# Layout changes of attention scores and probabilities: from VectorE block transposes to DMA transposes on SyncE's queue

## The chip, the cores and the metric

The kernel runs on one core of a Trainium2 chip. The metric is the device time of one execution in microseconds (us), by the slowest core, which here is the only one. An execution over 1.5% above the fastest of the same kernel counts as disturbed; undisturbed runs are compared throughout.

## The reference

The inputs are 2048 positions of 1024 features in bf16. Three things are computed from the same x and mixed by a gate of one value per position:

```python
def reference(A_x, A_wqkv, A_wo, B_x, B_w_gate, B_w_up, B_w_down, gate_w):
    # attention: 32 heads of 32, window of 8 positions, 2 apart (0, 2, .. 14 back)
    qkv = ...(x @ wqkv)                                  # 1024 -> 3 x 1024
    logits = einsum("bhsd,bhswd->bhsw", q, kg) * scale   # 8 logits per position and head
    attn = softmax(where(mask, logits, -1e9))
    a = einsum("bhsw,bhswd->bhsd", attn, vg) @ wo
    # feed-forward, 1024 -> 3584 -> 1024
    b = (gelu(x @ w_gate) * (x @ w_up)) @ w_down
    g = sigmoid((x * gate_w).sum(-1, keepdims=True))
    return g * a + (1 - g) * b
```

All weight products are large matrix products for TensorE. The window attention has only 8 logits per position and head, so it is done by VectorE, element by element.

## The kernel before

The positions come in four chunks of 512 (chunks 0 and 1 make the first half of the run, 2 and 3 the second), and the attention of each chunk in two halves of 256 (h = 0 to 7). Queries, keys and values lie as 128 partitions (32 heads times 4) by positions. VectorE multiplies and adds them to the partial scores of a half, 128 x 2048 values in bf16. The softmax wants positions on the partitions, so the scores are transposed, and the probabilities are transposed back before they multiply the values:

```python
# att_half: one half of a chunk
o = dve(2.24, taking("z", lambda: nc.vector.transpose(out=flat("z"), in_=xbuf[:, accs[h], :])), [("qk", h)],
        pre=xb_pre(), key=("acct", h))                       # scores: one "whole" transpose
# ... fold: adds the 4 partial sums of a head (VectorE), mask, maximum, subtraction
def exps():                                                  # ScalarE
    if a == 0:
        nc.scalar.activation(out=gates[c][0][:], in_=gates[c][2][:], func=ACT.Exp)
    nc.scalar.activation(out=lsb(), in_=lsb(), func=ACT.Exp, scale=scale)
# ... sums, reciprocal, gate (VectorE); spread: each probability copied 4 times (ScalarE)
for i in range(2):
    def back(i=i):                                           # probabilities: a pair of half-size transposes
        nc.vector.transpose(out=flat("ab")[:, i * n // 2:(i + 1) * n // 2],
                            in_=flat("e")[:, i * n // 2:(i + 1) * n // 2])
# ... products with V and their sums (VectorE), which write the attention output
```

All of this is woven into the matrix work of TensorE by a small scheduler that runs while the kernel is built. It gives every operation of each engine its place in a fixed order, from costs that it assumes. For transfers it assumes a common pipe and 2.2 us on top:

```python
LAT = 0.1
RATE = 340e3
...
if op.eng in ("SP", "POOL"):              # SyncE's and GpSimd's transfers
    nbytes, issue = op.cost
    self.clk[op.eng] = t + issue
    self.pipe = max(self.pipe, t) + nbytes / self.RATE
    op.end = self.pipe + 2.2
```

An engine that waits for one operation holds up all that stands behind it in its order; the lines below show it (ScalarE stands 8.04 us for one operation of VectorE's, with a copy behind it that TensorE needs). ScalarE's order holds the attention's exponentials and spreads as well as copies out of TensorE's result banks ("evacuations"); VectorE's order too. SyncE issues nearly all loads, in order: weights into a ring of 20 slots, and x by transposing loads. GpSimd issues the stores of computed weight combinations, 28 of "dforms", 8 of "oforms" and 56 of "fforms", nearly all in the first 230 us, and most outputs.

The loads of x for chunk 3 go into the buffer of chunk 0's values, so they wait for chunk 0's attention, and they stand in SyncE's order among the weights:

```python
xs = [... for z in lend[0:4]]             # x of chunk 3 lies in lend[3]
vT = [lend[3], lend[5], lend[1], lend[5]] # V of chunk 0 lies in lend[3]
def load_x(c, deps):
    deps = deps + ([[("acct", 1)], [("att", 0)]][c - 2] if c > 1 else [])
...
for b in range(2, NBLK):
    yield from load_block(0, b)
    if b >= XB:
        for c, k0 in ((2, 0), (2, 4), (3, 0), (3, 4))[b - XB:b - XB + 1]:
            yield from list(load_x(c, []))[k0:k0 + 4]
```

## Time and profile before

| | before |
|---|---|
| time, median of 3 (lowest to highest) | 732.13 us (731.79 to 732.85) |
| profiled span | 729.7 us |
| TensorE busy | 721.8 us, 99% |
| VectorE busy | 631.6 us, 87% |
| ScalarE, GpSimd busy | 314.9 us, 72.0 us |
| TensorE's clock granted | 1.00 |

The page of a profile has the busy time of each engine, then a row per engine of 40 slices of the span (here 18.2 us each) whose digits are busy tenths. "Busy" includes a matmul that runs slowly (for the same 3397 matmuls TensorE is busy 721.8 us before and 726.8 us after), so busy has to be compared with the matmuls' distance in time, as the prediction does. The lines themselves are shown in the prediction.

### The profile page before, as it was taken

Reading aid. Unit: us, or ns where it says so; the run is one execution under the profiler, and the core shown is the slowest. Engines: PE = TensorE matmul, PEld = TensorE weight load, DVE = VectorE, ACT = ScalarE, POOL = GpSimd, SP = SyncE. Lnnn points to the kernel's source line nnn. Section 1 sums busy time; section 2 is a strip of 40 time slices with the busy share of each in tenths; the row PEclk is TensorE's granted clock in tenths of the full one; section 3 lists DMA queues with packets and bytes.
Section 4 is the critical chain, followed back from the end, with each engine's and each line's share of the span. In section 5 each row is a group of like instructions: output and inputs, shape, how many; then the busy total and the mean of one; then the engine's idle time right before and its main releaser. Section 6 shows DMA issues by size and latency. Waiting matters only on the chain.

```text
span 729.7 us, 9971 instructions
## 1 busy us (share of the span) xinstructions
PE 721.8 (99%) x3397; PEld 356.0 (49%) x3397; DVE 631.6 (87%) x935; ACT 314.9 (43%) x532; POOL 72.0 (10%) x128
## 2 busy tenths in 40 slices
PE   8999999999999999999999998999999999999998
PEld 5666644444444444456665444444444444444443
DVE  2689999999999989999899999999999999969300
ACT  2333455558555561035652113576557654220110
POOL 2234422121210100000000001000000000001000
PEclk9999999999999999999999999999999999999999
DMA  9999965648892869943029999555455544899992
GB/s 302 333 325 363 380 200 170 187 139 212 213 227 74 280 194 326 314 162 116 29 89 300 358 302 333 165 150 155 147 159 147 156 151 145 303 304 336 323 303 104
DMA packets 151507, 163.73 MB, mean 224 GB/s; under 512 B 22944, under 2 KB 112032, under 8 KB 151456
## 3 DMA queue, kind: packets, MB, share of 16 engines
q1 hardware_dynamic: 142624, 135.30, 60.1%
q0 software_dynamic: 8544, 27.27, 10.1%
q8 instruction: 26, 0.43, 0.2%
q10 hardware_dynamic: 288, 0.52, 0.2%
q14 instruction: 25, 0.20, 0.1%
HBM read 129.50 MB, written 28.31 MB: 216 GB/s over the span
## 4 chain that ended last, share of the span: by engine, by line
PE 73%; issue 21%; DVE 2%; ACT 1%; DMA 1%; POOL 1%; POOLq 0%; ACTq 0%
PE ps L970 44%; PE ps L1117 17%; PE ps L473 11%; DVE xbuf L922 1%; POOL out_dram L1144 1%; DMA hT<-in_A_x_dram 0%; DVE xbuf L930 0%; PE ps L1212 0%; DMA out_dram<-ost 0%; DVE xbuf L935 0%; DVE ost L1191 0%; ACT ost L1152 0%; ACT L1058 0%; DVE xbuf L787 0%; PE ps L717 0%
## 5 line engine op out<-in xcount | busy, mean ns | idle before, releaser
L970 PEld LDWEIGHTS <-ring 128*128 128x128 bf16 x1568 | 153.2, 98 | 187.7 <-issue 3.5
L970 PE MATMUL ps<-lend,ring 128*128 128x512 bf16 x896 | 212.3, 379 | 2.2 <-ACT m L1024 2.1
L970 PE MATMUL ps<-tf,ring 128*128 128x512 bf16 x672 | 164.0, 379 | 0.0
L1117 PE MATMUL ps<-ring,hT 128*128 128x512 bf16 x708 | 160.7, 379 | 0.0
L1117 PEld LDWEIGHTS <-hT 128*128 128x128 bf16 x708 | 69.2, 98 | 83.3
L781 DVE TENSOR_TENSOR xbuf<-qo,lend 128x2048 bf16<-128x2048 bf16 x64 | 77.4, 1218 | 2.1 <-ACT lend L495 2.1
L922 DVE TENSOR_TENSOR xbuf<-xbuf,lend 128x2048 bf16<-128x2048 bf16 x64 | 77.4, 1218 | 0.1
L787 DVE TENSOR_TENSOR xbuf<-xbuf 128x2048 bf16<-128x2048 bf16 x56 | 68.2, 1218 | 0.2
L609 PEld LDWEIGHTS <-ring 128*128 128x128 bf16 x336 | 44.0, 131 | 28.7 <-DMA ring<-in_A_wqkv_dram 0.4
L473 PE MATMUL ps<-lend,ring 128*128 128x512 bf16 x256 | 56.3, 381 | 0.1
L1042 ACT ACTIVATE gl<-ps 128x512 bf16<-128x512 f32 x56 | 33.5, 598 | 51.5 <-PE ps L970 51.4
L999 ACT COPY ps<-ps 128x512 f32<-128x512 f32 x56 | 32.0, 571 | 54.9 <-PE ps L970 54.8
L1152 ACT ACTIVATE ost<-ps,omg 128x512 bf16<-128x512 f32 x16 | 11.0, 688 | 102.5 <-PE ps L1117 99.3
L1144 POOL DMA_DIRECT2D out_dram<-ost x24 | 13.0, 540 | 413.4 <-ACT ost L1152 319.4
L1117 PE MATMUL ps<-ring,qo 128*128 128x512 bf16 x192 | 49.3, 379 | 0.0
L473 PEld LDWEIGHTS <-ring 128*128 128x128 bf16 x256 | 36.8, 145 | 19.0 <-issue 0.7
L443 POOL DMA_DIRECT2D fforms<-ring x56 | 30.4, 544 | 132.4 <-DVE ring L435 120.6
L609 PE MATMUL ps<-lend,ring 128*128 128x512 bf16 x192 | 43.5, 379 | 0.0
L1014 DVE TENSOR_TENSOR hT<-hT,gl 128x1024 bf16<-128x1024 bf16 x56 | 38.4, 686 | 5.8 <-ACT hT L1011 4.5
L930 DVE TENSOR_TENSOR xbuf<-xbuf 128x1024 bf16<-128x1024 bf16 x64 | 41.9, 686 | 0.7
L1054 DVE TENSOR_TENSOR u<-ps,u 128x512 f32<-128x512 f32 x56 | 38.4, 686 | 4.6 <-PE ps L970 3.4
L1033 DVE TENSOR_TENSOR hT<-ps,m 128x512 bf16<-128x512 f32 x56 | 38.4, 686 | 4.0 <-PE ps L970 3.9
(106 smaller groups left out, 724.7 us busy)
## 6 DMA issues: line engine op xcount, KB each, us to landing
ring<-dforms SPq DMA_DIRECT2D x112, 256.0 KB, 4.9
ring<-in_B_w_down_dram SPq DMA_DIRECT2D x84, 256.0 KB, 4.1
ring<-in_B_w_gate_dram SPq DMA_DIRECT2D x56, 256.0 KB, 4.7
fforms<-ring POOLq DMA_DIRECT2D x56, 256.0 KB, 4.5
ring<-fforms SPq DMA_DIRECT2D x56, 256.0 KB, 3.9
ring<-in_B_w_up_dram SPq DMA_DIRECT2D x42, 256.0 KB, 3.3
ring<-in_A_wqkv_dram SPq DMA_DIRECT2D x40, 256.0 KB, 4.9
ring<-oforms SPq DMA_DIRECT2D x32, 256.0 KB, 5.6
```

The lines of the kernel that those rows point to most:

```text
L473: nc.tensor.matmul(banks[bk][:], lhsT=lhsT, rhs=xT(c, kt), start=(kt == 0), stop=(kt == KT - 1))
L609: nc.tensor.matmul(banks[bk][:], lhsT=lhsT, rhs=rhs[:, kt, :], start=(start and kt == 0), stop=(kt == KH - 1), skip_group_check=True)
L781: V(out=w3(box[t]), in0=q_b, in1=k_w, op=ALU.mult)
L787: V(out=w3(box[0]), in0=w3(box[0]), in1=w3(box[t]), op=ALU.add)
L922: return dve(tt(n), taking(("p", t), lambda: V(out=w3(box["p", t]), in0=w3(box["ab"]), in1=v_w, op=ALU.mult)), [("qkv", c, 2, t), abo] + ( ...
L930: V(out=s4(t)[:, t % 2], in0=w3(box["p", t])[:, 0:4], in1=w3(box["p", t])[:, 4:8], op=ALU.add)
L970: nc.tensor.matmul(banks[bk][:], lhsT=wv[:, k, fl * P:(fl + 1) * P], rhs=rhs[:, k, :], start=(start and k == 0), stop=(k == KH - 1), skip_ ...
L1014: yield dve(tt(2 * SC), lambda f=f: nc.vector.tensor_tensor(out=hT[:, :, f, :], in0=hT[:, :, f, :], in1=gl[f][:].rearrange("p (j s) -> p j ...
L1033: ev[f, "up2"] = dve(tt(SC, True), lambda f=f: nc.vector.tensor_tensor(out=hs(f, 1), in0=v3(banks[Bk[f]][:]), in1=v3(m5[f][:]), op=ALU.add ...
L1042: nc.scalar.activation(out=gl[f][:, SC:2 * SC], in_=banks[A[f]][:], func=ACT.Gelu_apprx_tanh)
L1054: e = dve(tt(SC, True), lambda f=f: nc.vector.tensor_tensor(out=u2[f][:], in0=banks[Dk[f]][:], in1=u2[f][:], op=ALU.add), [o, ev[f, "u2"]])
L1117: nc.tensor.matmul(banks[bk][:], lhsT=l, rhs=wv[:, i, :], start=(start and k == 0), stop=(q == last and i == 1), skip_group_check=True)
```

## The change

The intent: transposes are only data movement, VectorE is the second busiest engine, and SyncE's queue has room (its longest waits in sum, 198.0 and 82.3 us, are for TensorE to free a slot of the ring). VectorE's transpose (L844 before, 2306 ns for 128 x 2048) leaves blocks of 32 x 32 and the DMA transpose (L848 after) blocks of 128: so the two kernels index what they wrote. The positions of a half then lie in two blocks of 128 rather than eight of 32; the mask (7 memsets, not 28) and the gate values follow that order. The core of the diff:

```diff
-    SB = AC // 32
-    HQ = 32 // DL
+    SB = AC // P
@@ gate: clamped into a tile of its own, one matmul per 128 positions; no copies back from quarters @@
-            for q in range(4):
-                nc.vector.tensor_copy(out=omg[32 * q:32 * (q + 1), :],
-                                      in_=og[32 * q:32 * (q + 1), :].rearrange("p (j q) -> p j q", q=4)[:, :, q])
@@ attention @@
+        def rows(name):
+            return flat(name).rearrange("p (b s) -> p b s", s=P)
+
+        def turn(cols, fn, deps, **kw):
+            return Op("SP", (P * cols * 2, max(1.3, cols / 1000.0)), fn, deps, **kw)
...
-        o = dve(2.24, taking("z", lambda: nc.vector.transpose(out=flat("z"), in_=xbuf[:, accs[h], :])), [("qk", h)],
-                pre=xb_pre(), key=("acct", h))
+        o = turn(n, taking("z", lambda: nc.sync.dma_start_transpose(out=rows("z"), in_=xbuf[:, accs[h], :])), [("qk", h)],
+                 pre=xb_pre(), key=("acct", h))
...
-                for q in range(4):
-                    for wi in range(1, NWIN):
-                        nc.vector.memset(lsb()[32 * q:32 * q + DIL * wi, wi, 0:HQ], NEG)
-            o = dve(2.0, mask, [o])
+                for wi in range(1, NWIN):
+                    nc.vector.memset(lsb()[0:DIL * wi, wi, 0:H], NEG)
+            o = dve(0.5, mask, [o])
...
-                nc.vector.transpose(out=flat("ab")[:, i * n // 2:(i + 1) * n // 2],
-                                    in_=flat("e")[:, i * n // 2:(i + 1) * n // 2])
-            o = dve(1.16, taking("ab", back) if i == 0 else back, [es[i]], lag=0.6, pre=xb_pre() if i == 0 else None)
+                nc.sync.dma_start_transpose(out=rows("ab")[:, i * NWIN:(i + 1) * NWIN],
+                                            in_=flat("e")[:, i * n // 2:(i + 1) * n // 2])
+            o = turn(n // 2, taking("ab", back) if i == 0 else back, [es[i]], pre=xb_pre() if i == 0 else None)
```

More of the change, by code (lines that the diff above doesn't have):

```diff
@@ L729, in gate @@
         yield e
-        ez = small.tile([P, SC // 32], F32, tag="ez", bufs=2, name="ez")
+        zc = small.tile([P, NST], F32, tag="zc", bufs=2, name="zc")
+        ez = small.tile([P, NST], F32, tag="ez", bufs=2, name="ez")
         omg = small.tile([P, NST], F32, tag="omg", bufs=3, name="omg")
-        gates[c] = (ez, omg, zq)
+        gates[c] = (ez, omg, zq, zc)
     def gate_sum(c):
         i, free = bank_take()
-        zq = gates[c][2]
+        zq, zc = gates[c][2:4]
         def go():
             for q in range(4):
-                nc.tensor.matmul(banks[i][32 * q:32 * (q + 1), 0:SC // 32], lhsT=qsum[:], rhs=zq[:], start=True, stop=True,
+                nc.tensor.matmul(banks[i][32 * q:32 * (q + 1), 0:NST], lhsT=qsum[:],
+                                 rhs=zq[:].rearrange("p (j q) -> p j q", q=4)[:, :, q], start=True, stop=True,
                                  tile_position=(0, 32 * q), skip_group_check=True)
@@ L743, in gate_sum @@
         yield o
-        e = dve(0.1, lambda: nc.vector.tensor_scalar(out=zq[:], in0=banks[i][:, 0:SC // 32], scalar1=ZMAX, scalar2=-ZMAX,
+        e = dve(0.1, lambda: nc.vector.tensor_scalar(out=zc[:], in0=banks[i][:, 0:NST], scalar1=ZMAX, scalar2=-ZMAX,
                                                      op0=ALU.min, op1=ALU.max), [o], key=("zc", c))
@@ L749, in gate_tail @@
     def gate_tail(c):
-        ez, omg, og = gates[c]
+        ez, omg = gates[c][0:2]
         def tail():
-            nc.vector.tensor_scalar(out=og[:], in0=ez[:], scalar1=1.0, scalar2=1.0, op0=ALU.mult, op1=ALU.add)
-            nc.vector.reciprocal(out=og[:], in_=og[:])
-            for q in range(4):
-                nc.vector.tensor_copy(out=omg[32 * q:32 * (q + 1), :],
-                                      in_=og[32 * q:32 * (q + 1), :].rearrange("p (j q) -> p j q", q=4)[:, :, q])
-        yield dve(1.2, tail, [("ez", c)], lag=0.6, key=("omg", c))
+            nc.vector.tensor_scalar(out=omg[:], in0=ez[:], scalar1=1.0, scalar2=1.0, op0=ALU.mult, op1=ALU.add)
+            nc.vector.reciprocal(out=omg[:], in_=omg[:])
+        yield dve(0.3, tail, [("ez", c)], lag=0.6, key=("omg", c))
     accs = {}
@@ L878, in exps @@
             if a == 0:
-                nc.scalar.activation(out=gates[c][0][:], in_=gates[c][2][:], func=ACT.Exp)
+                nc.scalar.activation(out=gates[c][0][:], in_=gates[c][3][:], func=ACT.Exp)
             nc.scalar.activation(out=lsb(), in_=lsb(), func=ACT.Exp, scale=scale)
@@ L891, in att_half @@
                                 in1=gates[c][0][:, a * SB:(a + 1) * SB].rearrange("p (s o) -> p s o", o=1)
-                                .to_broadcast([P, SB, HQ]), op=ALU.mult), [("ez", c), o])
+                                .to_broadcast([P, SB, H]), op=ALU.mult), [("ez", c), o])
         yield o
```

## The prediction

> **What bounds the kernel now.** I read the busy rows of the page first, then the chain that ended last, then the groups by shape, then VectorE and SyncE in order of time. The page:
>
> ```profile
> PE 721.8 (99%) x3397; PEld 356.0 (49%) x3397; DVE 631.6 (87%) x935; ACT 314.9 (43%) x532; POOL 72.0 (10%) x128
> ...
> PE   8999999999999999999999998999999999999998
> ...
> DVE  2689999999999989999899999999999999969300
> ...
> DMA  9999965648892869943029999555455544899992
> ```
>
> TensorE is busy in every slice; VectorE is nearly as full, but only up to about 680 us. Busy TensorE need not be TensorE at its pace, so I take the pace from the chain of work, in order of time:
>
> ```profile
> 98.51 76.08 PE ps L970 x352
> ...
> 174.61 85.63 PE ps L970 x396
> ...
> 456.32 102.91 PE ps L970 x476
> ...
> 625.11 101.02 PE ps L1117 x468
> ```
>
> 76.08/352, 85.63/396, 102.91/476 and 101.02/468 are all 0.216 us per matmul of 512 columns, in the feed-forward and in the down projection alike: a uniform pace with no bubbles. By the groups there are 3296 such matmuls of 128 rows; at 0.216 they make 711.9 us. The small PE groups (transposes 3.6, warm-up 2.3, gate rows 2.3, gate sums 0.8 us) bring this to 720.9 us of the span of 729.7. The 8.8 us left are the load of x at the head (about 4), the last output's way out after the last matmul at 726.13 (3.6), and one stall:
>
> ```profile
> 454.44 0.69 DVE L1054 TENSOR_TENSOR u<-ps,u 128x512 f32<-128x512 f32 x1
> 455.05 0.42 DVE L939 TENSOR_TENSOR qo<-xbuf 128x512 bf16<-128x512 bf16 x1
> 455.16 0.63 ACT L1058 ACTIVATE gl<-u 128x512 bf16<-128x512 f32 x1 [3.76 <-DVE u L1054]
> ...
> 456.32 1.89 PE L970 MATMUL ps<-lend,ring 128*128 128x512 bf16 x8 [2.07 <-ACT m L1024]
> ```
>
> Here attention work stood in VectorE's order before an evacuation (L1054) for which ScalarE had waited 3.76 us; TensorE lost 2.07 us. Two smaller losses, at 174.6 and near 560, sum to about 0.2. So freeing VectorE can give at most some 2.3 us, 0.3%. No removal of VectorE work reaches 2%, since no matmul of weight is removed.
>
> [...] The trace has 2306 ns for 2048 columns, 144 ns per 128[...]; the transposing loads of x (512 rows by 128 columns) take about 1.28 us of SyncE. [...] those loads land a median 4.6 us after issue. [...] this trace's plain issues take about 0.4. No run here shows a transpose out of SBUF.
>
> **The change part by part.**
>
> ```profile
> L844 DVE STREAM_TRANSPOSE xbuf<-xbuf 128x2048 bf16<-128x2048 bf16 x8 | 18.5, 2306 | 0.1
> L913 DVE STREAM_TRANSPOSE xbuf<-xbuf 128x1024 bf16<-128x1024 bf16 x16 | 19.2, 1225 | 3.9 <-ACT xbuf L904 3.9
> L756 DVE COPY omg<-zq 32x4 f32<-32x4 f32 x16 | 2.6, 160 | 0.3
> ```
>
> Removed from VectorE: 18.5 + 19.2 us of transposes, 2.6 of gate copies, 21 of 28 mask memsets at 65 ns (1.4), and some 0.5 on narrower gate values: 42 us, so 632 becomes about 590. The other attention instructions keep their shapes.
>
> Added to SyncE: 8 transposes of 512 KB and 16 of 256 KB. The x loads are the nearest thing, here the first eight on SyncE in order of time (start, us):
>
> ```profile
> 25.54 13.02 SPq L313 DMA_TRANSPOSE lend<-in_A_x_dram  x8
> ```
>
> and, among the DMA issues (count, then median us from issue to landing):
>
> ```profile
> lend<-in_A_x_dram SPq DMA_TRANSPOSE x24, 4.6
> ```
>
> These eight took 1.63 us each beside other loads; the median of all 24 is 1.28. One of them moves 128 KB as 512 packets of 256 bytes. Scaling its 1.28 us by size gives 5.1 us for a whole and 2.6 for a half. [...] Its packets take a median 18 ns, so a whole (2048 packets over 16 engines) takes about 2.3 us of all DMA engines and a half 1.15: 37 us in all, about 5% of the span.
>
> SyncE can carry this. Its own waits are mostly for TensorE to free a slot of the ring of 20:
>
> ```profile
> SPq L342 <- PE ps L970: 198.0, 121, 12.8
> SPq L362 <- PE ps L1117: 82.3, 122, 3.5
> ```
>
> The weights run ahead by up to 20 pieces, at least 17 us in the down projection (4 matmuls a piece, 0.86 us). A block of 4 to 6 us on SyncE eats into that, not into TensorE.
>
> Latency gets longer. A whole should land about 6 to 7.5 us after it starts to issue, against 2.3 us on VectorE; the pair of halves about 6.5 against 2.45. That is some 4 us more, 16 times: 64 us more in the attention chain, against 42 us less VectorE work. VectorE has other work for most of it: before 680 us it idles only 46 us of 660, beyond the first 20 us (98.1 idle in all, less 43.8 after 680 and 8.1 before 20). Where it runs out, it stands. The scheduler in the kernel helps less than it thinks: it reckons 524288/340e3 + 2.2 = 3.7 us for a whole, so it places the fold 2 to 4 us early in VectorE's fixed order, with evacuations queued behind it.
>
> Deadlines of attention are loose. The end is the nearest: attention of the last chunk writes its output at 669.97, the combinations for the down projection follow, and the third product, which first needs one, starts about 687, four products of 3.88 us after 671.6. That is 15 us of slack. A late last half moves nothing.
>
> So what reaches TensorE are VectorE's stands inside the feed-forward: about 5 whole transposes (158, 252, 476, 550, 622) and 3 pairs (182, 498, 572). The stall above says an evacuation late by 3.8 us costs 2.1, so lateness under about 1.7 us costs nothing. If half of the 8 are late by 2 to 3 us, TensorE loses about 4 x 0.8 = 3 us. Sum: 732.1 - 2.0 (the old stall, likely gone with less work on VectorE) + 3 = 733.
>
> **The rivals.** (a) All is hidden: TensorE stays at 0.216 us and the stall goes; 729.5 to 730. For it: TensorE's pace never depends on attention. Against: VectorE's fixed order mixes attention waits with evacuations. (b) Transposes out of SBUF are much slower than x's, say 10 us a whole, or stand behind ring loads in the same queue, where DMA is 0.9 busy or more (down projections at 275-315, 395-450, 620-700). Then folds are 5 to 8 us late and each stand costs TensorE 3 to 5 us: 745 to 765. Against: packet sizes equal those of the x loads, and the feed-forward of the second half has DMA at half. (c) SyncE waits in order for VectorE's last sum or ScalarE's spread, and ring loads behind it starve TensorE: 735 to 745. Against: the ring's 17 us or more. (d) VectorE was the bound and 42 us come off the end: only if TensorE idled, which the 0.216 us rules out.
>
> **Range and chances.** The floor is 729.5, with half a microsecond for runs. Most weight lies at 730 to 737; a thin tail from (b) and (c) reaches beyond 740. Slower by 2% means over 746.8, which needs 14 us of new stalls, as in (b): 8%. Faster by 2%, under 717.5, would be below TensorE's own work: 1%.
>
> **What would show it.** VectorE near 590 us busy; matmuls still 0.216 us apart; [...]landing in 6 to 8; VectorE idle before the first fold and the first value product, released by DMA; TensorE idle of a few us in the feed-forward, released by ScalarE or VectorE. I am wrong if one transpose holds SyncE for 8 us or more, if TensorE waits on the ring's DMAs, or if the pace itself changes.

## The result, and the profile after

| | before | after |
|---|---|---|
| time, median (lowest to highest), same rounds | 732.19 us (731.79 to 732.85), 4 runs | 742.44 us (738.95 to 744.06), 4 runs |
| ratio, 95% interval | | 1.0133 (1.0093 to 1.0173) |
| profiled span | 729.7 us | 741.8 us |
| TensorE busy | 721.8 us | 726.8 us |
| VectorE busy | 631.6 us | 593.1 us |
| clock granted, mean | 1.00 | 0.992 |

A ratio here and below is the mean time of one kernel's fast runs over the mean of the other's in the same rounds, so it is not quite the ratio of the medians that are quoted. The kernel became 1.3% slower, outside the predicted range. The page after, busy times and then slices of 18.5 us:

```profile
PE 726.8 (98%) x3397; PEld 356.8 (48%) x3397; DVE 593.1 (80%) x874; ACT 315.0 (42%) x533; POOL 72.0 (10%) x128
...
PE   8999978999999999999999999999999999999998
...
DVE  2688597998999899996999898899989997794300
...
PEclk9999989999999999999999999999999999999999
DMA  9999996556996399993334999966576647899993
```

VectorE lost its 38.5 us, as meant. But TensorE has two slices below 9, the sixth and seventh (93 to 130 us), in the first of which its clock also dips, and VectorE shows a 5 in the fifth. The rest of the run looks as before. The span grew by 12.1 us: TensorE idles 741.8 - 726.8 = 15.0 us instead of 7.9 (7.1 more), and is busy 5.0 us longer with as many matmuls. What TensorE and VectorE waited for (total us, times, longest):

```profile
DVE xbuf L855 <- DMA xbuf<-xbuf: 15.3, 4, 9.9
...
PE ps L973 <- ACT ps L1002: 5.1, 1, 5.1
...
PE ps L973 <- ACT m L1027: 3.8, 2, 3.6
```

Two single waits for ScalarE, 8.7 us together, are the idle time that came in (the old stall of 2.07 us went), and one wait of VectorE's first fold (L855) for a transpose is the longest by far. In order of time (start, duration, engine; in brackets the idle time before, and what ended it):

```profile
63.70 5.67 SPq L848 DMA_TRANSPOSE xbuf<-xbuf  x1
...
81.37 0.69 DVE L855 TENSOR_TENSOR xbuf<-xbuf 128x1024 bf16<-128x1024 bf16 x1 [9.86 <-DMA xbuf<-xbuf]
...
84.98 0.63 ACT L883 ACTIVATE xbuf<-xbuf 128x512 f32<-128x512 f32 x1 [6.71 <-DVE xbuf L877]
...
96.56 1.04 ACT L907 COPY xbuf<-xbuf 128x1024 bf16<-128x1024 bf16 x1 [8.04 <-DVE xbuf L901]
...
99.20 5.23 SPq L916 DMA_TRANSPOSE xbuf<-xbuf  x2
...
99.94 0.60 ACT L1002 COPY ps<-ps 128x512 f32<-128x512 f32 x1
...
100.59 1.87 PE L973 MATMUL ps<-lend,ring 128*128 128x512 bf16 x4 [5.13 <-ACT ps L1002]
...
115.38 2.36 DVE L925 TENSOR_TENSOR xbuf<-xbuf,lend 128x2048 bf16<-128x2048 bf16 x2 [5.67 <-DMA xbuf<-xbuf]
...
118.37 0.63 ACT L1061 ACTIVATE gl<-u 128x512 bf16<-128x512 f32 x1 [5.57 <-DVE u L1057]
...
120.01 1.44 PE L973 MATMUL ps<-lend,ring 128*128 128x512 bf16 x3 [3.55 <-ACT m L1027]
```

In the kernel before, the same transpose and the same fold (L851 there), also in order of time:

```profile
61.69 2.32 DVE L844 STREAM_TRANSPOSE xbuf<-xbuf 128x2048 bf16<-128x2048 bf16 x1
...
67.11 0.69 DVE L851 TENSOR_TENSOR xbuf<-xbuf 128x1024 bf16<-128x1024 bf16 x1
```

This is the story of the first half of chunk 0. Its whole transpose is issued at 63.70 and has landed only at 81.37, 17.7 us later; the fold comes 14.3 us later than before. VectorE stands 9.86 us before the fold and then has a backlog. ScalarE's order has the exponential (L883) and the spread (L907) in front of the copy that seeds a result bank (L1002), so it stands 6.71 and 8.04 us for VectorE, and TensorE 5.13 us for that copy. The first pair of half transposes then does the same on VectorE's side: the value products (L925) wait 5.67 us with an evacuation (L1057) behind them, and TensorE stands 3.55 us.

Of the 5.0 us of longer busy time, 3.9 follow from the stalls. After the first stall the first five matmuls start 0.38 to 0.43 us apart; by the trace's clock records the clock was at half from 98.8 for 6.8 us and from 119.3 for 3.4 us. Matmuls between 100 and 140 us that started 0.3 to 0.6 us after the one before cost 3.9 us above 0.216 us each; before, none did there. What sets off such a spell of half clock was not shown: the second one began 2.8 us after TensorE had gone idle, and in experiment 9 a stall of 2.0 us was followed by 3.4 us at half clock, while the old stall of 2.07 us was not. So in this place each microsecond of standing cost about half a microsecond more (3.9 us for 8.7).

How the first transpose came to take so long shows in the windows (start and end, length, then busy time and number of instructions of TensorE, weight loads, VectorE, ScalarE and GpSimd; clock, DMA engines' busy share, GB/s). Before:

```profile
60.00:80.00 20.00, 20.00 (x100) 13.17 (x99) 19.52 (x59) 7.08 (x13) 8.58 (x13) 1.00 1.08 376
```

After:

```profile
60.00:80.00 20.00, 20.00 (x101) 13.21 (x100) 10.91 (x16) 6.54 (x12) 6.58 (x11) 1.00 1.13 225
...
100.00:120.00 20.00, 15.87 (x68) 6.52 (x68) 14.19 (x20) 8.58 (x16) 5.10 (x8) 0.84 1.07 244
```

The DMA engines are as busy as before, at 40% fewer bytes per second. Counting packets in the trace between 67.1 and 80.2 us gives 2048 packets of 256 bytes, the transpose, and 295 of 4096 bytes of GpSimd's queue, which took 404 ns each on average, though the median is 164 (before 63 us and after 81 us the averages are 162 to 201). I call this the crawl. Around 170 us, with few packets of GpSimd's, a whole took 3.0 us from first to last packet. The typical transpose isn't slow, as the row of all eight shows (duration of the issue and landing, least/median/greatest):

```profile
L848 SPq DMA_TRANSPOSE xbuf<-xbuf x8: 1906/2422/5672, 63.7 to 617.2; - x8
...
DMA to landing us min/median/max: 4.2/5.0/17.7
```

### The profile page after: what moved, and what is told of

Its sections match the earlier page's. It is cut to its first block, busy times and chain, and to the rows that moved or that the text cites.

```text
span 741.8 us, 9968 instructions
## 1 busy us (share of the span) xinstructions
PE 726.8 (98%) x3397; PEld 356.8 (48%) x3397; DVE 593.1 (80%) x874; ACT 315.0 (42%) x533; POOL 72.0 (10%) x128
## 3 DMA queue, kind: packets, MB, share of 16 engines
q0 software_dynamic: 8544, 27.27, 11.1%
## 4 chain that ended last, share of the span: by engine, by line
PE 80%; DVE 4%; ACT 2%; issue 1%; DMA 1%; DVEq 0%; ACTq 0%
PE ps L973 40%; PE ps L1120 29%; PE ps L608 10%; DVE xbuf L779 1%; DMA xbuf<-xbuf 1%; DVE u L1057 1%; DVE ring L434 1%; DVE xbuf L785 0%; DVE hT L1036 0%; ACT hT L1014 0%; DVE hT L1017 0%; ACT ps L1002 0%; ACT lend L494 0%; ACT m L1027 0%; ACT L1061 0%
## 5 line engine op out<-in xcount | busy, mean ns | idle before, releaser
L973 PE MATMUL ps<-lend,ring 128*128 128x512 bf16 x896 | 215.3, 383 | 9.0 <-ACT ps L1002 5.1
L925 DVE TENSOR_TENSOR xbuf<-xbuf,lend 128x2048 bf16<-128x2048 bf16 x64 | 77.7, 1221 | 10.2 <-DMA xbuf<-xbuf 10.1
L472 PE MATMUL ps<-lend,ring 128*128 128x512 bf16 x256 | 56.9, 384 | 0.1
L1002 ACT COPY ps<-ps 128x512 f32<-128x512 f32 x56 | 32.0, 572 | 55.3 <-PE ps L973 55.2
L1017 DVE TENSOR_TENSOR hT<-hT,gl 128x1024 bf16<-128x1024 bf16 x56 | 38.6, 689 | 12.6 <-ACT hT L1014 11.8
L1057 DVE TENSOR_TENSOR u<-ps,u 128x512 f32<-128x512 f32 x56 | 38.5, 688 | 10.7 <-PE ps L973 10.1
L442 POOL DMA_DIRECT2D fforms<-ring x56 | 30.4, 543 | 140.6 <-DVE ring L434 135.9
L608 PE MATMUL ps<-lend,ring 128*128 128x512 bf16 x192 | 43.5, 379 | 0.0
L1036 DVE TENSOR_TENSOR hT<-ps,m 128x512 bf16<-128x512 f32 x56 | 38.5, 687 | 3.2 <-PE ps L973 3.1
```

The costliest lines, as they stand in the source:

```text
L472: nc.tensor.matmul(banks[bk][:], lhsT=lhsT, rhs=xT(c, kt), start=(kt == 0), stop=(kt == KT - 1))
L608: nc.tensor.matmul(banks[bk][:], lhsT=lhsT, rhs=rhs[:, kt, :], start=(start and kt == 0), stop=(kt == KH - 1), skip_group_check=True)
L925: return dve(tt(n), taking(("p", t), lambda: V(out=w3(box["p", t]), in0=w3(box["ab"]), in1=v_w, op=ALU.mult)), [("qkv", c, 2, t), abo] + ( ...
L973: nc.tensor.matmul(banks[bk][:], lhsT=wv[:, k, fl * P:(fl + 1) * P], rhs=rhs[:, k, :], start=(start and k == 0), stop=(k == KH - 1), skip_ ...
L1017: yield dve(tt(2 * SC), lambda f=f: nc.vector.tensor_tensor(out=hT[:, :, f, :], in0=hT[:, :, f, :], in1=gl[f][:].rearrange("p (j s) -> p j ...
L1036: ev[f, "up2"] = dve(tt(SC, True), lambda f=f: nc.vector.tensor_tensor(out=hs(f, 1), in0=v3(banks[Bk[f]][:]), in1=v3(m5[f][:]), op=ALU.add ...
```

## The experiments

The theory after the result: the loss is made in the opening (60 to 130 us) alone; the first whole transpose crawls beside GpSimd's stores; the late result reaches TensorE through the fixed orders of VectorE and ScalarE. The rivals: the loss is spread over the run (folds a bit late everywhere); SyncE's own traffic or its being held by long issues is what counts; the scheduler's too short estimate is the cause, so that a truthful one would mend it; or any way of waiting longer costs this much, with or without the crawl. Line numbers move by a few lines from kernel to kernel.

**1. Chunk 0 alone on VectorE, and chunk 0 alone by DMA.** The two kernels choose the path by chunk, with layout, mask and gate following it:

```diff
-    SB = AC // P
+    VEC = (0,)                     # second kernel: VEC = (1, 2, 3)
+    def blk(c):
+        return 32 if c in VEC else P
...
-        o = turn(n, ... nc.sync.dma_start_transpose(out=rows("z"), in_=xbuf[:, accs[h], :]) ...
+        o = dve(2.24, ... nc.vector.transpose(out=flat("z"), in_=xbuf[:, accs[h], :]) ...) if c in VEC else turn(n, ...
```

> The changed kernel, but the two halves of chunk 0 keep VectorE's transposes; the other six halves use DMA. Theory A (the loss is made in the first half of chunk 0, where the first transposes land 14 to 18 us after issue): both stalls near 95 and 116 us and both spells of the half clock go, and the old stall near 455 us stays away: 729.5 to 731, granted clock 1.00. Rival B (the longer chain and SyncE's extra work cost a little in every half): six of eight halves still pay, 737 to 741.

Measured: 731.56 us against 731.7 of before; ratio 0.9998 (0.998 to 1.0017); the result is correct. In the slices no stall of the opening is left:

```profile
PE   8999999999999999999999999999999999999998
```

> The reverse: only chunk 0 uses DMA transposes, chunks 1 to 3 stay on VectorE. Theory A: the whole loss is still there, 741 to 745, with the slow landings near 64 and 100 us, and the old 2 us stall near 455 perhaps back. Rival B: two of eight halves pay, 733 to 736.

Measured: 740.7 us against 731.7; ratio 1.0126 (1.0104 to 1.0149); correct. TensorE's longest wait is the one known from above, and longer (the first whole's packets ran 15.6 us here):

```profile
PE ps L990 <- ACT ps L1019: 8.5, 1, 8.5
```

What follows: the whole loss is in chunk 0. The DMA transposes of chunks 1, 2 and 3, six wholes and six pairs, cost nothing and gain nothing, so the rival of a loss spread over the run falls. The first kernel's median came out just above the 729.5 to 731 that I had hoped for, and the old stall had not stayed away (1.1 us at 454.7): even without a loss there is no gain to see.

**2. One transpose by itself beside other traffic.** A small kernel, wrong as a computation, transposes 128 x 2048 in SBUF from SyncE's queue, while another queue stores or loads 16 pieces of 256 KB:

```diff
+    phase(0, lambda: None)
+    phase(1, lambda: stores(nc.gpsimd, 1))
+    phase(2, lambda: stores(nc.scalar, 2))
+    phase(3, lambda: stores(nc.sync, 3, 4))
+    phase(4, lambda: loads(nc.gpsimd))
+    phase(5, lambda: loads(nc.scalar))
+    phase(6, lambda: loads(nc.sync, 8))
+    phase(7, lambda: stores(nc.gpsimd, 7), lambda k: nc.sync.dma_start(out=zt[k]..., in_=xin[k][:]))    # a plain copy of the tile
+    phase(8, lambda: stores(nc.gpsimd, 8), lambda k: nc.sync.dma_start(out=zt[k]..., in_=B_w_up...))    # a load
```

> No part of the kernel: one DMA transpose of 128 by 2048 out of SBUF at a time, with different traffic beside it, the result wrong on purpose. Theory C: alone, behind SyncE's own stores or loads, and beside loads on GpSimd's queue its packets take 2.3 to 5 us; beside GpSimd's stores 9 us or more; beside stores on ScalarE's queue something between; a plain copy of the same tile beside GpSimd's stores stays under 5 us. Rival D: all traffic slows it by about as much per byte, the plain copy too. Issue by SyncE 1.9 to 3 us when alone.

Measured, from the trace's packet records:

| beside | first to last packet, us | issue on SyncE, us |
|---|---|---|
| nothing | 2.60 | 1.99 |
| GpSimd's stores | 12.35 | 5.51 |
| the same, but a plain copy of the tile | 3.08 | 0.53 |
| ScalarE's stores | 4.03 | 3.70 |
| SyncE's own 4 stores before it | 2.60 | 1.83 |
| GpSimd's loads | 11.89 | 9.73 |
| ScalarE's loads | 8.84 | 5.33 |
| SyncE's own 8 loads before it | 2.92 | 4.17 |

What follows: traffic of another queue stretches the transpose to between 1.5 and nearly 5 times its time (4.03 to 12.35 us for 2.60), GpSimd's most. A plain copy of the same 512 KB beside the same stores takes 3.08 us, so not every transfer crawls; but it moves in 128 packets of 4096 bytes, the transpose in 2048 of 256, and a plain copy in small packets was not tried. About SyncE's own queue little is shown: its 4 stores had ended 0.8 us before the transpose was issued, and its 8 loads overlapped it for 1.1 us (0.3 us more from the first packet on, 1.9 from the issue on). The load of phase 8 was issued at 1.65 us, out of its place, and shows nothing. For the loads of GpSimd I had expected under 5 us, and that missed: it isn't about stores. In the phase with GpSimd's stores 511 packets of 4096 bytes ran among the 2048 of 256 bytes, one for about every four.

**3. What sets the crawl.** The same with neighbours that write other row sizes:

```diff
+    # sixteen stores of 256 KB beside one transpose: GpSimd with rows of 2 KB, 512 bytes, 4 KB; then four only
+    # ScalarE with rows of 2 KB, 512 bytes, 4 KB; then SyncE's own sixteen
```

> The same measuring kernel, wrong on purpose, with the neighbour's packet size changed: GpSimd stores in rows of 2 KB (as before), 512 bytes and 4 KB, then ScalarE stores in the same three, then only four GpSimd stores, then SyncE's own sixteen stores. If one packet of the neighbour goes between every four of the transpose (as the first measurement counted), 512-byte neighbours let it finish in 3 to 5 us on either queue, 4 KB on ScalarE's queue takes 9 us or more, and four stores cost about 5 us in all. If it is GpSimd's queue as such, its 512-byte rows still take 9 us or more and ScalarE's 4 KB stay at 4.

Measured, first to last packet: beside GpSimd's stores 11.1 us with rows of 2 KB, 14.0 with 512 bytes, 6.2 with 4 KB; beside ScalarE's 4.2, 4.4 and 10.0; behind SyncE's own sixteen 2.6. The packet records show that the test did less than I meant. GpSimd's packets were 4096 bytes whatever the row; only ScalarE's changed (2048, 512 and 4096 bytes). With rows of 4 KB GpSimd's stores ran out 2.2 us before the transpose ended: in the 4.0 us beside them only 525 of its 2048 packets moved, so 6.2 us is no shorter crawl. The last packet of the four stores began 1.2 us before the transpose's first, so that phase (2.6 us) shows a transpose alone; of SyncE's sixteen nearly all had moved before it too. What remains: beside a neighbour the transpose moved between 1.75 packets (GpSimd, rows of 4 KB) and 9.75 (ScalarE, 2 KB) for each one of the neighbour's. So "one for every four" is not the rule, and the rule stays open.

**4. The stores of GpSimd moved to SyncE's queue,** in the kernel after and in the kernel before:

```diff
-                o = Op("POOL", (n * P * NW * 2, 0.8), lambda f=f: nc.gpsimd.dma_start(out=dd[:, f, r0:r0 + n, :], ...
+                o = Op("SP", (n * P * NW * 2, 0.45), lambda f=f: nc.sync.dma_start(out=dd[:, f, r0:r0 + n, :], ...
-                    yield Op("POOL", (P * GR * 2, 0.6), lambda b=b, f=f: nc.gpsimd.dma_start(out=fdram[b]...
+                    yield Op("SP", (P * GR * 2, 0.45), lambda b=b, f=f: nc.sync.dma_start(out=fdram[b]...
```

> The changed kernel, but the stores of the combined weights (84 + 8 + 56 minus none: all of dforms, oforms and fforms) are issued by SyncE and not by GpSimd, so that GpSimd's queue is empty while the first transposes run. Theory C (a transpose crawls when GpSimd's queue interleaves 4 KB packets with it): from first to last packet the first whole takes 3 to 5 us instead of 13, the first pair 3 to 5 instead of 12.6, and the time falls to 731 to 736, unless SyncE's waits for VectorE's forms hold back loads. Rival D (any loaded DMA system or the queue's own backlog slows it): still over 9 us in packets, and 738 or more.

Measured: 742.66 us against 731.7; ratio 1.0149 (1.0126 to 1.0173); correct. (The count of stores in that text is garbled: it is 28, 8 and 56.) The crawl is gone: the first whole's packets take 3.2 us and the pair's 4.3. Yet TensorE stands elsewhere:

```profile
PE ps L973 <- DVE ring L434: 4.2, 2, 3.7
PE ps L973 <- DVE hT L1036: 3.1, 1, 3.1
```

> A control for the run with the stores on SyncE: the kernel before, transposes on VectorE, with the same stores moved from GpSimd to SyncE. If moving the stores costs time by itself (SyncE waits in order for VectorE's forms and holds back loads), this is well above before: 738 to 742, and the transposes in that run cost only the small rest. If it stays at 731 to 733, the run with stores on SyncE lost its time to the transposes in spite of the short packets, and theory C is incomplete.

Measured: 730.47 us against 732.97; ratio 0.9977 (0.9961 to 0.9992). So moving the stores does no harm by itself, and the loss in the other kernel belongs to the transposes. My hope that ending the crawl would end the loss fell with this. It cures the one stall it was blamed for, and others appear, at 104 and 109 and near 248 us (for weight combinations, L434; see 7). That SyncE now carries the stores itself and the transposes don't crawl also speaks against the rival that SyncE's own traffic is what counts.

**5. The scheduler told the truth.** The fold and the value products are planned 10 us late for h = 0 and 2.5 us for the others:

```diff
-        o = dve(tt(2 * CW), taking("w", fold), [o], pre=xb_pre())
+        slow = 10.0 if h == 0 else 2.5
+        o = dve(tt(2 * CW), taking("w", fold), [o], lag=slow, pre=xb_pre())
...
-                       [("qkv", c, 2, t), abo] + ([("halo", c, 2)] if c else []), lag=0.5, pre=xb_pre())
+                       [("qkv", c, 2, t), abo] + ([("halo", c, 2)] if c else []), lag=slow, pre=xb_pre())
```

> The changed kernel, with only the scheduler told that its transposes land late (10 us in the first half, 2.5 us in the others), so that VectorE's fixed order puts other work ahead of the work that waits for them. If a late landing hurts only because evacuations are queued behind the waiting instruction, the stalls near 95 and 116 shrink and it runs at 732 to 737 although the crawl stays at 12 us or more. If the length of the chain itself hurts, 740 to 745 as before.

Measured: 745.83 us against 732.97; ratio 1.0184 (1.0156 to 1.0213); correct. The first whole's packets took 16.8 us, more than what was planned for; TensorE stood 7.7 us for ScalarE up to 102 and 3.5 us near 250. With these figures telling the scheduler did not help, so the rival of a mere wrong estimate is not supported; a plan with a longer delay still was not tried.

**6. Transposes and GpSimd's stores kept apart in time.** Every transpose of h = 0 waits for the stores issued before it, and later stores wait for it:

```diff
+        if op.kind == "turn":
+            deps = deps + [o for o, _ in self.pooled[-4:]]
+        elif op.eng == "POOL":
+            deps = deps + [o for o, _ in self.turned[-2:]]
... and the same as semaphore waits on the instructions; kind="turn" for h == 0 only
```

> The changed kernel with waits added: the first half's three transposes (one whole, two halves) start only when GpSimd's last four DMAs have landed, and GpSimd's next DMA is issued only when they have landed. Nothing else differs but the order that the kernel's scheduler derives. Theory C (the crawl comes from sharing the DMA engines with GpSimd's queue): their packets take 3 to 4.5 us instead of 13, the stalls near 95 and 116 us shrink below 2 us in sum, no or one short spell of the half clock, 731 to 735. Rival D (load in SyncE's own queue, or the longer latency in itself): packets still over 9 us or the stalls still there, 739 or more.

Measured: 754.47 us against 732.97; ratio 1.0301 (1.0282 to 1.032); correct. No crawl (2.9 and 2.8 us) and no stall in the opening. But the transposes themselves were held back until 104 and 136 us, so chunk 0's attention ended at 249.5, and TensorE stood between 235 and 260 us:

```profile
PE ps L984 <- DVE ring L444: 12.3, 1, 12.3
PE ps L984 <- DMA ring<-in_B_w_gate_dram: 7.6, 1, 7.6
```

The test was too rough for its question, but it showed a deadline that I had overlooked. SyncE's order has the loads of x for chunk 3 here; they overwrite chunk 0's values and so wait for chunk 0's attention, and the weights wait behind them.

**7. Only GpSimd waits.** The same without the wait of the transposes for stores:

```diff
+        if op.eng == "POOL":
+            deps = deps + [o for o, _ in self.turned[-2:]]
```

> The changed kernel with one wait added: GpSimd's next DMA is issued only when the first half's transposes have landed. Unlike the run that also held the transposes back, these start at about 64 and 99 us as in the changed kernel. Theory C (the crawl beside GpSimd's queue makes the opening's stalls): the whole lands within 9 us of issue instead of 17.7 and the pair within 8 instead of 14, TensorE's idle time between 80 and 125 us falls from 8.7 us to under 3, and it runs at 732 to 737. Rival E (any landing later than the scheduler reckons stalls the opening just as much, or the held-back stores do): 739 or more.

Measured: 739.01 us against 731.17; ratio 1.0097 (1.0079 to 1.0115); correct. The first whole's packets take 3.4 us and the pair's 4.1, they land at most 8.9 and 7.7 us after issue, and TensorE has no stall from 80 to 220 us, as the theory had it; the time is still the rival's (739 or more). What is left, beside 0.8 us near 465, is one stall, in order of time:

```profile
203.33 15.95 SPq L320 DMA_TRANSPOSE lend<-in_A_x_dram  x4
...
221.65 11.88 SPq L320 DMA_TRANSPOSE lend<-in_A_x_dram  x4
...
244.89 1.46 PE L982 MATMUL ps<-tf,ring 128*128 128x512 bf16 x3 [6.66 <-DVE ring L442]
```

Eight loads of x that take 1.3 us each otherwise occupy SyncE for 27.8 us, since each waits for a piece of chunk 0's attention (its last output is at 236.0, against 222.8 in the kernel before), and the weight combinations (L442) starve behind them. So the crawl and the stalls of the opening go together, and this deadline is a second cost of a longer chain. In the kernel after the last output is later still, at 239.0, without such a stall; but TensorE is some 12 us behind there, so the opening's loss probably hid this one. That was not tested. Stalls for weight combinations between 248 and 260 us appear in experiments 4, 5, 6 and 8 too.

**8. Scores alone and probabilities alone by DMA.** The kernel before, with one of the two changed. The layouts of the two no longer match, so both are wrong; the second is off by 0.16. Only their times count.

```diff
 # first kernel
-        o = dve(2.24, ... nc.vector.transpose(out=flat("z"), in_=xbuf[:, accs[h], :]) ...
+        o = turn(n, ... nc.sync.dma_start_transpose(out=rows("z"), in_=xbuf[:, accs[h], :]) ...
 # second kernel
-                nc.vector.transpose(out=flat("ab")[:, i * n // 2:(i + 1) * n // 2], ...
+                nc.sync.dma_start_transpose(out=rows("ab")[:, i * NWIN:(i + 1) * NWIN], ...
```

> The kernel before with one part of the change: only the scores are transposed by DMA (8 wholes), the probabilities by VectorE; layouts do not match, so the result is wrong on purpose. If the two stalls of the opening are separate, one by each part, this has the first stall (about 5 us near 95 us, and a spell of the half clock) and not the second: 737 to 740. If the second follows from the first, all of it is here: 741 to 744. If only the pair matters: 731 to 733.

Measured: 749.98 us against 731.17; ratio 1.0253 (1.0235 to 1.027). The first whole's packets took 17.2 us.

```profile
PE ps L976 <- ACT ps L1005: 12.7, 1, 12.7
PE ps L976 <- DVE ring L435: 5.6, 1, 5.6
```

That is more than any case of the expectation: the second of these, near 257 us, was in none of them.

> The other part alone: probabilities by DMA (16 halves), scores by VectorE; wrong on purpose. If the stalls are separate: about 3.5 us of stall near 110 us with a short spell of half clock, 734 to 738. If the second stall only followed from the first, 731 to 733.

Measured: 728.62 us against 731.17; ratio 0.9964 (0.9949 to 0.9978), clock 1.00, and no stall: beyond the head, TensorE waits nowhere longer than 0.2 us. The loss comes with the scores' transposes. The probabilities' alone gain about 2.5 us, near the size of the old stall; that stall also goes in experiment 10 by a mere change of order, so the gain isn't shown to be the transposes'. Their first pair, issued at 89.9, took 4.6 us from first to last packet, not 12.6 as in the kernel after: the whole was not late, the pair was issued earlier and did not crawl. Lateness alone doesn't decide, though: with chunk 0 alone by DMA (1) and in the last run of 10 the whole crawled, and the pair after it took 4.2 and 3.5 us.

**9. Chunk 0 on VectorE and the stores on SyncE,** the edits of 1 and 4 together, to see whether their gains add up:

```diff
+    VEC = (0,)
-                o = Op("POOL", (n * P * NW * 2, 0.8), ... nc.gpsimd.dma_start ...
+                o = Op("SP", (n * P * NW * 2, 0.45), ... nc.sync.dma_start ...
```

> Two results put together, as a candidate that may beat both kernels: chunk 0 transposes on VectorE, chunks 1 to 3 by DMA, and the form stores on SyncE instead of GpSimd (which alone made the kernel before 0.2% faster). If the gains add up, 729 to 730.5 and faster than before by 0.2 to 0.4%. If the DMA transposes of chunks 1 to 3 give nothing, as before with its stores moved: about 0.998 of before. If SyncE's order suffers: above before.

Measured: 733.53 us against 731.17; ratio 1.0033 (1.0013 to 1.0053); correct. They don't: a stall of 2.0 us for VectorE appears near 275 us, and one of 1.2 us for ScalarE is back near 459.

**10. The loads of x for chunk 3 put behind all weights of the first half,** in the kernel of experiment 7, in the kernel before and in the kernel after:

```diff
-                for c, k0 in ((2, 0), (2, 4), (3, 0), (3, 4))[b - XB:b - XB + 1]:
+                for c, k0 in ((2, 0), (2, 4))[b - XB:b - XB + 1]:
                     yield from list(load_x(c, []))[k0:k0 + 4]
+        yield from load_x(3, [])
```

> The run in which GpSimd waits for the first half's transposes, with one more edit: the loads of x for the last chunk, which overwrite chunk 0's V and so wait for its attention, stand in SyncE's order behind the last feed-forward weights and not among them. Theory F (the 6.7 us stall near 240 us is made by weights queued behind those loads): that stall goes, TensorE idles under 1 us between 80 and 260, and the kernel runs at 728.5 to 731, 0.2 to 0.4% faster than before, all transposes by DMA. Rival G (VectorE's fixed order makes that stall, whatever SyncE does): still 736 or more.

Measured: 746.17 us against 731.89; ratio 1.0197 (1.0175 to 1.0219); correct. The stall near 245 us is gone, as it should be if those loads made it. But two new ones appeared, at 357.7 and 419 us; the first stands behind a fold for which VectorE waited 4.29 us for a transpose:

```profile
PE ps L617 <- DVE lend L678: 4.0, 1, 4.0
PE ps L1130 <- DVE hT L1098: 3.8, 1, 3.8
```

> Control: the kernel before with only that reordering of the last chunk's loads. Theory F: before had no stall there, so 730 to 732.5, within 0.2% of before. If it gains as much as the run above does, the gain of that run is not the transposes'.

Measured: 729.53 us against 731.89; ratio 0.9969 (0.9957 to 0.9982); correct. No stall is left beyond the head, that of 2.07 us near 455 included:

```profile
PE ps L474 <- DMA ring<-in_A_wqkv_dram: 0.7, 1, 0.7
```

This version, with VectorE's transposes, beats both kernels, by 0.3% and 1.7% (1 - 729.53/742.44, across rounds). Why the old stall went was not looked into; the edit shifts the order of all that follows.

> The changed kernel with only that reordering, the crawl left in. Theory C with F: the opening's stalls stay (8 to 10 us of TensorE idle between 80 and 125 us and two spells of the half clock), so 739 to 743. If it falls under 735, the opening's crawl was not the cause of the loss.

Measured: 749.97 us against 731.89; ratio 1.0239 (1.0215 to 1.0263); correct. The first whole crawled for 19.1 us and TensorE stood 9.4 us; and in the last chunk a fold waited 12.87 us and the value products 10.13 us for transposes, so that TensorE stood for the last chunk's attention:

```profile
PE ps L1121 <- DVE qo L943: 6.5, 2, 3.4
```

The runs that have the first whole by DMA, ordered by its packets' time:

| kernel | first whole, us | TensorE's stall near 100 us for ScalarE's seed copy |
|---|---|---|
| both transposes apart in time (6) | 2.9 | none |
| stores on SyncE (4) | 3.2 | none (others of 1.6 and 3.1) |
| GpSimd waits (7) | 3.4 | none |
| GpSimd waits, x late (10) | 5.2 | 1.1 |
| the kernel after | 13.0 | 5.1 |
| chunk 0 alone by DMA (1) | 15.6 | 8.5 |
| scheduler told (5) | 16.8 | 7.7 |
| scores alone by DMA (8) | 17.2 | 12.7 |
| the kernel after, x late (10) | 19.1 | 9.4 |

The stall near 100 us follows the crawl. Its removal is worth at most part of the loss, since a chain of longer transposes moves deadlines elsewhere (experiments 4, 7 and 10).

## Why the prediction was wrong

The point predicted was 733 us with 728.8 to 740.5 as the range (in the words above a floor of 729.5, most weight at 730 to 737 and a thin tail beyond 740); 742.44 lies 1.9 us above it.

- **TensorE is the bound, at 0.216 us per matmul, so freeing VectorE gains next to nothing.** Right. VectorE went from 631.6 to 593.1 us (about 590 was said), and the kernel with the transposes of chunks 1 to 3 by DMA is as fast as before (0.9998).
- **The old stall goes.** Right: it is not among TensorE's waits after.
- **Issue on SyncE, scaled by size from an x load: 5.1 us for a whole and 2.6 for a half.** Too long: the medians are 2.42 and 1.30 us, the shortest 1.91 and 1.23 in the kernel after (a whole alone 1.99, experiment 2). An x load's 1.28 us does not scale by size to a transpose out of SBUF.
- **Landing in 6 to 7.5 us.** An estimate of mine: too long for the usual transpose (medians 5.0 and 4.2), and the size that failed where it counted: 17.7 us for the first whole and 13.8 us at most for a half. I worked from the packet's median of 18 ns, which is right even in the crawl, and took the DMA engines' time as if the transpose had them to itself.
- **"So what reaches TensorE are VectorE's stands inside the feed-forward: about 5 whole transposes ... and 3 pairs", 3 us.** This is the step that failed. My list of stands began at 158 us. I left out the first whole, due near 64 us, and the first pair, although the slices of before have the DMA engines at 9 tenths from 55 to 91 us, with GpSimd's stores among their work. Outside the opening the stands cost about 0.6 us by the windows of 20 us, not 3; inside it they cost 8.7 us of idleness (4.54 and 4.13 in the windows from 80 and from 100 us), and about 4 us of half clock, a term that the sum did not have at all. Together that is some 12.6 us where the sum has 3.
- **"Deadlines of attention are loose."** Wrong. I had looked at the last chunk's output only. ScalarE's fixed order puts the first exponential and spread in front of the feed-forward's first evacuations, and chunk 3's x waits for chunk 0's attention. The second did not bite in the kernel after (TensorE's waits for weight combinations are 0.2 us), but it made the stall of experiment 7, which went when those loads were moved (10), and by its place that of 6. The 15 us of the last chunk were enough in the kernel after and not in the last run of experiment 10.
- **The rivals.** (b) was nearest in kind, a whole of 10 us or more with evacuations late behind it, but I put it in the down projections and gave SyncE's own ring loads as the cause. The trace put it in the opening, and with the stores on SyncE's own queue the crawl was gone (4). (c), a starved ring, is absent after, but real in 6 and 7. (a) and (d) fell; the run with chunk 0 on VectorE (731.56) comes near (a), without its gain.
- **"I am wrong if one transpose holds SyncE for 8 us or more."** It held it for 5.67 us at most in the kernel after, so that sign did not show; with chunk 0 alone by DMA it was 11.88 us. The third sign, a change of the pace itself, did: 10.2 us at half clock.
- **A sum.** The parts named for the 8.8 us make 9.9 (4, 3.6, 2.07 and 0.2), so "about 4" at the head was too much. It does not touch the result.

What is shown: the loss lies in chunk 0 (experiment 1), with the scores' transposes (8); other queues' traffic makes a transpose 1.5 to nearly 5 times as long (2); with GpSimd's traffic held back beside it the stalls of the opening go (7), though with that traffic moved to SyncE others come there (4). What stays open: what rule sets the crawl's length (3), whether it is the transposing or the small packets that make it crawl (2), and whether some order of this kernel with all transposes by DMA reaches the time of before. None of the seven variants run with chunk 0 fully by DMA did; the best was 739.01 us.

## What to carry to other kernels

When work is moved from an engine to a DMA, look up the place of each single transfer in the run, and what other queues move in that moment; a median latency (here 5.0 us) says nothing about the one that is on a fixed order's path (17.7). Then list every consumer of the late result, including those that only wait for its buffer, with all that stands behind them in the same engine's order. Where TensorE is already at its pace, freeing another engine has little upside to pay for such a risk (here one stall of 2.07 us).
